# A fused attention, low-rank mix and MLP kernel: float32 low-rank products, copies moved to VectorE, earlier weight decoding, a reordered last hidden layer

## The chip, the cores and the metric

One core of one Trainium2 chip. The metric is device time of one execution in microseconds, the median of the runs.

## The reference

For batch 4, 12 heads, sequence 448 and head size 64, causal attention; its output, with the heads side by side, is x of shape (4, 448, 768). Then a low-rank mix along the sequence and an MLP:

```python
scores = q @ k.T / sqrt(64), masked above the diagonal
attn = exp(scores - max) / (sum + 1e-9);  x = attn @ v
h = x.transpose(0, 2, 1) @ U @ V                 # U (448, 32), V (32, 448)
u = x + h.transpose(0, 2, 1)
out = u + maximum(u @ w_ch1, 0) @ w_ch2          # (768, 3072), (3072, 768)
```

U, V, w_ch1 and w_ch2 arrive as float64 words.

## The kernel before, in words

Everything is computed transposed: x lies as six tiles of 128 channels by 448 positions per batch. Three stages follow one another.

**Attention** (`attention`, line 843 and on). 48 heads pass through a software pipeline of iterations n. `PLAN` (line 47) lists the steps of an iteration in issue order, each with a lag: step (name, lag) works at iteration n on head n - lag. The names: ld loads q and k (L201), ma and mb are the scores (L214; two tiles side by side on the row halves 0 to 63 and 64 to 127), x3 to x0 subtract the maximum (VectorE, L228), e3 to e0 the exponentials (ScalarE, L242), nr the inverse sums (VectorE, L249), n3 to n0 the normalising (POOL, L255), p1, p2, p0 the transposes (L266), h1, h0, h2 the copies of the transposed probabilities out of PSUM (`transposed`, through `copy` L167, engine by the table `ENG`, L39), v the product with v (L281, two heads side by side on column halves), vc its copy. xp transposes x back (L311), xh and xl copy it as a high fp32r part (ScalarE, L315) and the remainder (VectorE, L320); lp is the product with U (`low_rank`, L328: eight fp32r matmuls of 256 columns against a stack of U's high and low parts), lh and ll bring it into the tile y as high part and remainder (L337, L341), once per four heads. `mix` (L346, L347) multiplies y with V's high and low parts, one channel tile per iteration from iteration 14 on for batch 0 and 26 on for batch 1; `mix_sum` (L351) adds it to x, and POOL splits the sum into fp32r parts (L171, L175).

Beside it run steps at fixed iterations: V and U are loaded and decoded from 64-bit words by `low_rank_weights` at iterations -1, 3, 5, 6 (`VU_AT`), and the first two MLP weight blocks are loaded at 10 and 11 and decoded at `START` - 8, 6, 4, 3, 2, that is 26, 28, 30, 31, 32 (`W_AT`). A decoding is two ScalarE passes and three VectorE passes (`decode_bits`, L152 to L156), a sum on POOL (L160) with a store of the block into `kept` (L386), and a split into fp32r parts on ScalarE and VectorE (L178, L179). Such a step is issued right after the first step of its iteration.

**Mixed stage** (`mlp`, lines 402 to 449). From iteration 34 on the MLP of batches 0 and 1 runs, with the rest of the attention steps dealt out between its products at an even rate: products hf (L415) and of (L440), each weight block decoded two blocks ahead. A float32 product is made as three fp32r products of high and low parts.

**Strassen stage** (`strassen`, line 807 and on). Batches 2 and 3 use a seven-product scheme on quads of blocks, with the kept weights loaded again. A quad is (kind, part, k): kind 1 is the hidden layer (9 matmuls per product), kind 2 the output layer (6). There are six parts; hidden quads are called a, b, a2 (part, 0 or 1), output quads k0, k1, k3. `order` (line 725 and on) writes the product sequence; an item (q, n, m) is half of product n. `results` adds each finished product into `xb` (or `r` for kind 1) on VectorE (L461); `hidden` turns a finished hidden quad into operands H, by rounds of VectorE subtractions (tmp, L461), ScalarE casts (L469) and VectorE remainders (h). `prepare` does the same for weights (sw, wsp; L461, L584). `layer` holds the rounds of `hidden`, two per product. `stored` (lines 761 to 767) stores a quad's four tiles in the last part after its seventh product. This stage is ordered by a planner that follows the program order but moves instructions on an engine's queue by its own estimate of readiness; in the stages before the order of the program is kept on every engine.

Of the kernel before, what the change touches and what calls it, by code (L numbers as in the profile page):

```python
# [19 lines left out]
P = 128  # L20
# [19 lines left out]
    "h0": "A", "h1": "A", "h2": "A", "vc": "A",  # L40
# [16 lines left out]
VU_AT = (-1, 3, 5, 6)  # L57
# [8 lines left out]
W_AT = (8, 6, 4, 3, 2)  # L66
# [3 lines left out]
def attention_mix_mlp(ctx: ExitStack, tc: tile.TileContext, qk, v, w1, w2, vu, out):  # L70
# [42 lines left out]
    um_s = const.tile([CP, NT, 4, R], F32R, name="um_s")  # L113
    vm_h = const.tile([P, S], F32R, name="vm_h")
    vm_l = const.tile([P, S], F32R, name="vm_l")
    xn_h = const.tile([CP, NT, 2 * P], F32R, name="xn_h")
    xn_l = const.tile([CP, NT, 2 * P], F32R, name="xn_l")
# [63 lines left out]
    def low_rank_weights(step):  # L181
        if step == 0:
            st["vu"] = load_words(vu, VCOLS)
        elif step == 1:
            st["vua"] = decode_bits(st["vu"], VCOLS)
        elif step == 2:
            decode_sum(st.pop("vu"), st["vua"], VCOLS)
        else:
            a = f(st.pop("vua"))
            split(a[:, :S], vm_h, vm_l)  # L190
            u = a[:CP, S:].rearrange("p (s r) -> p s r", s=NT)
            for i in (0, 2):
                split(u, um_s[:, :, i, :], um_s[:, :, i + 1, :])
# [119 lines left out]
    def natural_high(b, c):  # L313
        cs = slice((c % 2) * P, (c % 2 + 1) * P)
        nc.scalar.copy(xn_h[:, :, cs], st["xn", b, c])  # L315

    def natural_low(b, c):
        cs = slice((c % 2) * P, (c % 2 + 1) * P)
        o = st.pop(("xn", b, c))
        nc.vector.tensor_tensor(xn_l[:, :, cs], o, f(xn_h[:, :, cs]), op=ALU.subtract)  # L320
# [15 lines left out]
    def low_rank_high(b, n):  # L336
        nc.scalar.copy(st["y", b][:, n * 2 * P : (n + 1) * 2 * P], st["yo", b, n])  # L337

    def low_rank_low(b, n):
        y, o = st["y", b][D:, n * 2 * P : (n + 1) * 2 * P], st.pop(("yo", b, n))  # L340
        nc.vector.tensor_tensor(y, o[D:], f(y), op=ALU.subtract)  # L341
# [391 lines left out]
    for p in range(NPART):  # L733
# [150 lines left out]
    with tc.manual_schedule():  # L884
        constants()
        early = [(n, low_rank_weights, (i,)) for i, n in enumerate(VU_AT)]
        early += [(10, load_w, (0,)), (11, load_w, (1,))]
        for n, steps in zip(
# [90 lines left out]
```

## Time and profile before

| | |
|---|---|
| three runs | 913.18 us median (911.19 to 915.44) |
| the profiled execution | 909.54 us, span 907.6 us |
| busy share of the span | TensorE 97%, weight loads 83%, VectorE 73%, ScalarE 54%, POOL 35% |
| mean granted TensorE clock | 0.995 of full speed |

A share of busy time is a mean over stages with different limits; TensorE's ends are modelled, and a record that waits inside a run of merged records counts as busy. So the share alone does not tell what an added operation costs; the rows below are read stage by stage.

### The profile page before, as it was taken

The page shows a single profiled execution, that of the slowest core. Times are in us where ns is not written, and L with a number is a line of the kernel's source. Part 1 is how long each engine was busy: PE and PEld are TensorE (multiplying, and loading weights), DVE is VectorE, ACT ScalarE, POOL GpSimd, SP SyncE. Part 2 cuts the span into 40 slices and gives each one's busy share as a digit, 9 for nine tenths or more (in the row PEclk, how much of TensorE's full clock was granted, in tenths as well). Part 3 has the DMA queues.
Part 4 walks back from the last instruction along what each step waited for, and adds up shares of the span by engine and source line. Part 5 has one row for each costly group of instructions (what it writes and reads, how often), then busy time and mean ns, then how long its engine had stood idle before and what let it go on. Part 6 is the DMA issues. An engine that isn't in the chain of part 4 may idle for free.

```text
span 907.6 us, 13761 instructions
## 1 busy us (share of the span) xinstructions
PE 877.9 (97%) x4728; PEld 749.6 (83%) x4728; DVE 663.6 (73%) x1320; ACT 486.6 (54%) x1050; POOL 314.4 (35%) x342
## 2 busy tenths in 40 slices
PE   6999998999999999999999999899999998999998
PEld 4776766888888888878889999898999897898987
DVE  4656677565665756657568788789888988989885
ACT  5998987654555544455444545364453634445350
POOL 3547576221222322223214425323424323322420
PEclk9999999999999999999999999999999999999999
DMA  8584565354454455433434446612211321202103
GB/s 209 135 216 128 151 156 155 125 174 139 135 179 134 157 165 163 139 116 119 153 105 156 157 157 208 203 42 71 70 52 35 94 59 42 72 24 85 47 1 122
DMA packets 51285, 110.02 MB, mean 121 GB/s; under 512 B 5392, under 2 KB 26896, under 8 KB 51216
## 3 DMA queue, kind: packets, MB, share of 16 engines
q1 hardware_dynamic: 51216, 109.14, 39.7%
q8 instruction: 38, 0.62, 0.3%
q14 instruction: 31, 0.25, 0.1%
HBM read 84.74 MB, written 24.38 MB: 120 GB/s over the span
## 4 chain that ended last, share of the span: by engine, by line
PE 78%; DVE 10%; ACT 7%; issue 3%; DMA 1%; POOL 1%; SPq 0%; DVEq 0%; ACTq 0%; POOLq 0%
PE hf L415 20%; PE of L440 19%; PE sa L647 14%; PE se L647 6%; PE s L214 5%; PE pv L281 5%; PE t L266 4%; ACT p L242 3%; PE sb L647 3%; DVE h L461 2%; DVE tmp L461 2%; DVE sw L461 1%; DVE wsp L461 1%; PE y L328 1%; DVE p L228 1%
## 5 line engine op out<-in xcount | busy, mean ns | idle before, releaser
L440 PE MATMUL of<-g,wsp 128*128 128x448 f32 x864 | 183.8, 368 | 0.0
L461 POOL TENSOR_TENSOR wsp<-wld,wsp 128x512 fp32r<-128x512 f32 (+1 forms) x60 | 104.1, 1745 | 219.2 <-ACT wsp L584 113.2
L440 PEld LDWEIGHTS of<-g,wsp 128*128 128x128 f32 x864 | 160.2, 188 | 18.3 <-issue 2.1
L160 POOL TENSOR_TENSOR wa<-wld 128x768 int32<-128x768 int32 (+1 forms) x49 | 73.2, 1494 | 289.0 <-issue 159.6
L242 ACT ACTIVATE p<-p,m 112x448 f32<-112x448 f32 x192 | 99.7, 523 | 59.6 <-DVE m L228 59.3
L255 POOL TENSOR_SCALAR p<-p,r 112x448 f32<-112x448 f32 x192 | 96.7, 521 | 67.7 <-DVE r L250 40.5
L647 PE MATMUL sa<-h,wsp 128*128 128x448 f32 x432 | 98.5, 367 | 1.4 <-DVE xb L461 0.7
L647 PE MATMUL sa<-uch,wsp 128*128 128x448 f32 x288 | 89.6, 371 | 7.5 <-ACT r L668 4.8
L415 PE MATMUL hf<-u,wsp 128*128 128x448 f32 x432 | 94.9, 370 | 0.0
L415 PE MATMUL hf<-wsp 128*128 128x448 f32 x432 | 94.0, 368 | 0.5 <-ACT pt L167 0.5
L228 DVE CUSTOM_DVE_ANT_0 p<-s,mask 112x448 f32<-112x448 f32 x192 | 75.8, 443 | 20.0 <-PE s L214 19.1
L443 DVE TENSOR_TENSOR xa<-of,xa 128x448 f32<-128x448 f32 x96 | 58.7, 619 | 42.9 <-PE of L440 42.3
L647 PEld LDWEIGHTS sa<-h,wsp 128*128 128x128 f32 x432 | 80.7, 188 | 9.9 <-DVE xb L461 2.0
L415 PEld LDWEIGHTS hf<-u,wsp 128*128 128x128 f32 x432 | 79.8, 188 | 10.7 <-issue 3.8
L415 PEld LDWEIGHTS hf<-wsp 128*128 128x128 f32 x432 | 80.0, 188 | 9.9 <-issue 0.9
L424 DVE SCALAR_TENSOR_TENSOR g<-hf,g 128x448 fp32r<-128x448 f32 x48 | 29.9, 623 | 71.9 <-ACT g L423 71.8
L214 PE MATMUL s<-qk 64*112 64x448 f32 (+3 forms) x384 | 70.5, 444 | 6.6 <-DMA qk<-in_qk_dram 4.2
L178 ACT CAST wsp<-wa 128x768 fp32r<-128x768 f32 x48 | 40.0, 833 | 68.4 <-POOL wa L160 50.9
L423 ACT ACTIVATE g<-hf 128x448 fp32r<-128x448 f32 x48 | 26.1, 543 | 84.0 <-PE hf L415 83.8
L167 ACT COPY pt<-t 112x336 f32<-112x336 f32 x144 | 62.1, 472 | 10.7 <-PE t L266 10.7
L647 PEld LDWEIGHTS sa<-uch,wsp 128*128 128x128 f32 x288 | 54.0, 188 | 16.2 <-ACT r L668 8.3
L584 ACT CAST wsp<-wld 128x512 fp32r<-128x512 f32 (+1 forms) x60 | 41.7, 703 | 47.1 <-PE sa L647 35.7
(92 smaller groups left out, 1598.4 us busy)
## 6 DMA issues: line engine op xcount, KB each, us to landing
wld<-in_w_dram SPq DMA_DIRECT2D x48, 768.0 KB, 4.7
qk<-in_qk_dram SPq DMA_DIRECT2D x96, 224.0 KB, 4.1
kept<-wa SPq DMA_DIRECT2D x48, 384.0 KB, 2.6
wld<-kept SPq DMA_DIRECT2D x24, 384.0 KB, 3.3
wld<-kept SPq DMA_DIRECT2D x72, 128.0 KB, 2.5
v<-in_v_dram SPq DMA_DIRECT2D x24, 224.0 KB, 4.8
out_dram<-xa SPq DMA_DIRECT2D x12, 224.0 KB, 2.3
out_dram<-xb SPq DMA_DIRECT2D x12, 224.0 KB, 1.9
```

Source lines behind the costliest of these rows:

```text
L160: nc.gpsimd.tensor_tensor(a.bitcast(I32), t[:, :n, 1].bitcast(I32), t[:, :n, 0].bitcast(I32), op=ALU.add)
L167: nc.scalar.copy(o, i)
L214: nc.tensor.matmul(o[:, : (i + 1) * CP], t[r, 0, i * CP : (i + 1) * CP], t[r, 1, : (i + 1) * CP], start=True, stop=True,)
L228: nc.vector.tensor_tensor_reduce(out=st["p", b, h][:, POFF[i] : POFF[i] + n], in0=st.pop(("o", b, h, i))[:, :n], in1=mask[:, S - n :], sca ...
L242: nc.scalar.activation(pi, pi, AF.Exp, bias=m[:, i : i + 1], scale=-1.0, accum_out=l[:, i : i + 1])
L255: nc.gpsimd.tensor_scalar(pi, pi, r[:, i : i + 1], 1.0, op0=ALU.mult, op1=ALU.mult)
L281: nc.tensor.matmul(o[j * D : (j + 1) * D, kt * CP : S], v[:, kt, j, :], pt[:, n0 : n0 + S - kt * CP], start=(kt == 0), stop=(kt == NT - 1),)
L415: nc.tensor.matmul(o, a[:, cs], m, start=(kc + n == 0), stop=(kc + n == NC + 1))
L440: nc.tensor.matmul(o, a[:, cs], m, start=(fc + n == 0), stop=(fc + n == FC + 1))
L443: nc.vector.tensor_tensor(x, o, x, op=ALU.add)
L461: (nc.vector if e == "V" else nc.gpsimd).tensor_tensor(o, a, b, op=op)
L647: nc.tensor.matmul(st[bank, q], a, b, start=(n in FIRST and ms[0] == 0 and k == 0), stop=(n in LAST and end and k == len(steps) - 1), skip ...
```

## The change

`ENG` gives h2 to VectorE. The low-rank part keeps U, V, x and y in plain float32: steps xl and ll, the corrections of the high parts, go; lp makes four matmuls of 112 x 32 by 112 x 256 in place of eight of 112 x 128; mix makes one matmul of 32 x 128 by 32 x 448 in place of two of 128 x 128. V and U are loaded at iteration 1 and decoded at 4, 5 and 6; the first two weight blocks are loaded at 3 and 5 and decoded at 8, 9, 10, 11 and 13. The hidden operands of the last part go into tiles of the pool that held the split u of batches 2 and 3, and the second hidden quad of the last part moves from the last part into the one before. Each output tile is stored after the product that completes it.

```diff
 ENG = {
-    "h0": "A", "h1": "A", "h2": "A", "vc": "A",
+    "h0": "A", "h1": "A", "h2": "V", "vc": "A",
...
-    ("xl", 4), ("lv", 1), ("n1", 1), ("xp", 3), ("n0", 1), ("lh", 5),
-    ("ll", 5), ("e1", 0), ("nr", 0),
+    ("lv", 1), ("n1", 1), ("xp", 3), ("n0", 1), ("lh", 5),
+    ("e1", 0), ("nr", 0),
...
-VU_AT = (-1, 3, 5, 6)
+VU_AT = (1, 4, 5, 6)
...
-W_AT = (8, 6, 4, 3, 2)
+W_AT = (8, 9, 10, 11, 13)
...
-            split(a[:, :S], vm_h, vm_l)
-            u = a[:CP, S:].rearrange("p (s r) -> p s r", s=NT)
-            for i in (0, 2):
-                split(u, um_s[:, :, i, :], um_s[:, :, i + 1, :])
+            nc.vector.tensor_copy(vm, a[:R, :S])
+            nc.vector.tensor_copy(um, a[:CP, S:].rearrange("p (s r) -> p s r", s=NT))
...
-        o = st["yo", b, n] = bank("y")[:, : 2 * P]
+        o = st["yo", b, n] = bank("y")[:R, : 2 * P]
         for s in range(NT):
-            for t in (xn_h, xn_l):
-                nc.tensor.matmul(
-                    o,
-                    um_s[:, s].rearrange("p a r -> p (a r)"),
-                    t[:, s, :],
-                    start=(s == 0 and t is xn_h),
-                    stop=(s == NT - 1 and t is xn_l),
-                )
+            nc.tensor.matmul(o, um[:, s], xn[:, s, :], start=(s == 0), stop=(s == NT - 1))
...
-        ys = st["y", b][:, c * P : (c + 1) * P]
-        nc.tensor.matmul(o, ys, vm_h, start=True, stop=False)
-        nc.tensor.matmul(o, ys, vm_l, start=False, stop=True)
+        nc.tensor.matmul(o, st["y", b][:, c * P : (c + 1) * P], vm, start=True, stop=True)
...
         def operand(key):
+            if q[1] == NPART - 1:
+                if not last:
+                    last.extend(p_uc.tile([P, 7, S], F32R, tag=f"u{x}{k}", name="h") for x in "hl")
...
-        if p + 1 < NPART:
+        if p + 2 == NPART:
+            b2 = (1, p + 1, 1)
+            order((a2, 0), (b, 5), (a2, 1), (b, 6), (a2, 2), (a2, 3))
+            order((k0, 0, 0), (k0, 3, 0), (a2, 4), (k0, 1, 0), (a2, 5), (k0, 0, 1), (k0, 3, 1), (a2, 6))
+            order((k0, 2), (k0, 1, 1), (b2, 0), (k0, 4), (b2, 1), (k0, 6), (b2, 2), (k0, 5), (b2, 3), (b2, 4))
+            order((k1, 0), (b2, 5), (k1, 3), (b2, 6), (k1, 2), (k1, 1), (k1, 6), (k1, 4))
...
         else:
-            order((b, 5), (b, 6), (k0, 0, 0), (k0, 3, 0), (k0, 1, 0), (k1, 0, 0), (k1, 3, 0), (k1, 1, 0))
-            order((k0, 0, 1), (k0, 3, 1), (k0, 2), (k0, 1, 1), (k0, 6), (k0, 4), (k1, 0, 1), (k1, 3, 1))
...
+            order((k0, 0), (k0, 3), (k2, 5), (k0, 2), (k0, 1), (k0, 6), (k0, 4), (k1, 0), (k1, 3))
+            order((k0, 5), (k1, 2), (k1, 1), (k1, 6), (k1, 4))
         order((k3, 0), (k3, 3), (k1, 5), (k3, 2), (k3, 1), (k3, 6), (k3, 4))
...
-    def stored(q):
+    def stored(q, n):
         if q[0] == 2 and q[1] == NPART - 1:
-            for d in range(2):
-                for b in range(2):
+            for d, b in {1: ((0, 0),), 4: ((1, 1),), 5: ((0, 1),), 6: ((1, 0),)}.get(n, ()):
...
-                    if q[0] == 2 and q[2] == NC // 2 - 1 and q[1] + 1 < NPART:
+                    if q[0] == 2 and q[2] == NC // 2 - 1 and q[1] + 2 < NPART:
                         layer.extend(hidden((1, q[1] + 1, 0)))
+                    elif q == (1, NPART - 1, 1):
+                        layer.extend(hidden((1, NPART - 1, 0)) + hidden(q))
...
-        early += [(10, load_w, (0,)), (11, load_w, (1,))]
+        early += [(3, load_w, (0,)), (5, load_w, (1,))]
...
-            early += [(START - n, step, a) for step, a in steps]
+            early += [(n, step, a) for step, a in steps]
+        early.sort(key=lambda e: e[0])
```

## Rows read from the trace of the kernel before

**Rows 1.** The chain of waits that ended last, from the page (its part 4): shares of the span by engine. PE is TensorE, PEld its weight loads, DVE VectorE, ACT ScalarE, POOL GpSimd, SP SyncE; a q marks an engine's sequencer.

```profile
PE 78%; DVE 10%; ACT 7%; issue 3%; DMA 1%; POOL 1%; SPq 0%; DVEq 0%; ACTq 0%; POOLq 0%
```

**Rows 2.** The windows view: each stretch in us from the start, its length, then busy us (x instructions) of PE, PEld, DVE, ACT and POOL, the mean granted TensorE clock as a share of full speed, the DMA share and GB/s.

```profile
0.00:35.40 35.40, 26.18 (x165) 18.41 (x165) 17.28 (x78) 25.68 (x82) 15.57 (x33) 0.95 0.74 182
35.40:59.80 24.40, 24.13 (x186) 19.04 (x184) 14.08 (x65) 22.59 (x75) 11.57 (x24) 1.00 0.76 201
59.80:110.50 50.70, 50.23 (x374) 37.44 (x372) 31.26 (x136) 45.64 (x148) 33.06 (x60) 1.00 0.56 140
110.50:151.90 41.40, 37.15 (x255) 25.68 (x253) 31.87 (x99) 34.38 (x105) 29.78 (x46) 0.96 0.59 159
151.90:577.20 425.30, 423.28 (x2229) 363.73 (x2228) 285.23 (x519) 210.95 (x397) 123.43 (x122) 1.00 0.47 152
800.00:858.00 58.00, 57.35 (x280) 52.16 (x279) 52.92 (x82) 26.87 (x46) 16.74 (x10) 1.00 0.19 55
858.00:907.60 49.60, 44.00 (x210) 38.45 (x208) 35.83 (x55) 15.48 (x26) 11.25 (x7) 0.99 0.15 56
```

**Rows 3.** The timeline of iteration 20, from the end of 19 to the start of 21, TensorE's rows: start us, duration us, engine, line, operation, out<-in and count; runs of like instructions are merged.

```profile
85.85 0.47 PE L346 MATMUL hm<-vm_h,y 128*128 128x448 f32 x1
...
86.45 2.11 PE L281 MATMUL pv<-pt,v 112*64 112x448 f32 x16
...
88.49 1.17 PE L266 MATMUL t<-ident,p 112*112 112x112 f32 x10
...
89.59 1.20 PE L214 MATMUL s<-qk 64*112 64x448 f32 x8
...
90.72 0.38 PE L328 MATMUL y<-xn_h,um_s 112*128 112x256 f32 x1
...
91.78 0.60 PE L311 MATMUL xt<-ident,xa 128*112 128x128 f32 x4
...
92.21 1.12 PE L266 MATMUL t<-ident,p 112*112 112x112 f32 x10
```

**Rows 4.** The groups by line with shapes kept apart, whole execution: shapes, count, busy us and mean ns of one, idle before.

```profile
L281 PE MATMUL pv<-pt,v 112*64 112x448 f32 x96 | 26.9, 577 | 1.4 <-ACT pt L167 1.2
...
L281 PE MATMUL pv<-pt,v 112*64 112x112 f32 x96 | 11.1, 265 | 0.0
...
L347 PE MATMUL hm<-vm_l,y 128*128 128x448 f32 x24 | 8.8, 366 | 0.0
```

**Rows 5.** The timeline of TensorE in the mixed stage, around one mix.

```profile
252.56 0.37 PE L346 MATMUL hm<-vm_h,y 128*128 128x448 f32 x1
...
252.96 0.45 PE L266 MATMUL t<-ident,p 112*112 112x112 f32 x3
```

**Rows 6.** The same groups by line as in group 4: a copy of transposed probabilities on ScalarE, a mask pass on VectorE.

```profile
L167 ACT COPY pt<-t 112x336 f32<-112x336 f32 x96 | 42.4, 441 | 5.9 <-PE t L266 5.9
...
L228 DVE CUSTOM_DVE_ANT_0 p<-s,mask 112x336 f32<-112x336 f32 x48 | 24.1, 502 | 0.0
```

**Rows 7.** Iterations 26 to 33: three rows of the timeline (ScalarE, VectorE, TensorE), and two windows with the columns of group 2.

```profile
113.43 0.90 ACT L152 ACTIVATE wa<-wld 128x768 f32<-128x768 f32 x1
...
139.71 2.10 DVE L153 TENSOR_SCALAR wa<-wa 128x768 f32<-128x768 f32 x1
...
141.42 3.77 PE L281 MATMUL pv<-pt,v 112*64 112x448 f32 x16
...
138.00:141.00 3.00, 1.34 (x7) 0.62 (x5) 2.06 (x4) 3.00 (x9) 1.52 (x3) 1.00 0.35 80
141.00:143.00 2.00, 2.00 (x8) 0.80 (x10) 1.97 (x2) 1.02 (x3) 2.00 (x4) 0.68 0.63 158
```

**Rows 8.** The timeline at the start: ScalarE's decoding of V and U, and TensorE's pv that goes on after it.

```profile
17.28 0.71 ACT L152 ACTIVATE wa<-wld 128x576 f32<-128x576 f32 x1
...
19.41 2.10 PE L281 MATMUL pv<-pt,v 112*64 112x448 f32 x14 [1.18 <-ACT pt L167]
```

**Rows 9.** From the page: the DMA issues of weight blocks (KB each, median us to landing), and ahead of it the costliest POOL group of the decoding (columns as in group 4).

```profile
L160 POOL TENSOR_TENSOR wa<-wld 128x768 int32<-128x768 int32 (+1 forms) x49 | 73.2, 1494 | 289.0 <-issue 159.6
...
wld<-in_w_dram SPq DMA_DIRECT2D x48, 768.0 KB, 4.7
```

**Rows 10.** The groups by line of VectorE alone, 858 to 884 us: operands of the last part's hidden quads, and results of the quads before.

```profile
L461 DVE TENSOR_TENSOR h<-tmp,h 128x896 fp32r<-128x896 f32 x4 | 4.4, 1103 | 0.9 <-ACT h L469 0.9
L461 DVE TENSOR_TENSOR h<-r,h 128x896 fp32r<-128x896 f32 x2 | 3.2, 1616 | 0.0
...
L461 DVE TENSOR_TENSOR tmp<-r,tmp 128x448 f32<-128x448 f32 x4 | 2.5, 617 | 0.1
L461 DVE TENSOR_TENSOR h<-r,h 128x448 fp32r<-128x448 f32 x2 | 1.9, 975 | 1.2 <-ACT h L469 1.2
L461 DVE TENSOR_TENSOR xb<-sa,xb 128x448 f32<-128x448 f32 x3 | 1.8, 614 | 0.0
```

**Rows 11.** The timeline of the last part: TensorE after two of its waits.

```profile
875.00 0.47 PE L647 MATMUL se<-uch,wsp 128*128 128x448 f32 x1 [0.77 <-DVE r L461]
...
902.65 1.50 PE L647 MATMUL sa<-h,wsp 128*128 128x448 f32 x6 [0.72 <-DVE xb L461]
```

**Rows 12.** The stores of the last quad, from the view of one tensor (out_dram): duration ns min/median/max, then first and last start in us.

```profile
L765 SPq DMA_DIRECT2D out_dram<-xb x1: 333/333/333, 902.6 to 902.6; - x1
...
L765 SPq DMA_DIRECT2D out_dram<-xb x1: 333/333/333, 904.8 to 904.8; - x1
```

More of the change, by code (lines that the diff above doesn't have):

```diff
@@ L112, in attention_mix_mlp @@
     mask = const.tile([CP, S], F32, name="mask")
[L113 to L117, printed above, removed]
+    um = const.tile([CP, NT, R], F32, name="um")
+    vm = const.tile([R, S], F32, name="vm")
+    xn = const.tile([CP, NT, 2 * P], F32, name="xn")
     def f(ap):
@@ L311, in x_natural, with natural, low_rank_out @@
             nc.tensor.transpose(o[:, s, :], x[:, s * CP : (s + 1) * CP], ident)
-    def natural_high(b, c):
+    def natural(b, c):
         cs = slice((c % 2) * P, (c % 2 + 1) * P)
[L315 to L320, printed above, removed]
+        nc.scalar.copy(xn[:, :, cs], st.pop(("xn", b, c)))
     def low_rank(b, n):
         if n == 0:
-            st["y", b] = p_y.tile([P, DM], F32R, tag="y", name="y")
-        o = st["yo", b, n] = bank("y")[:, : 2 * P]
+            st["y", b] = p_y.tile([R, DM], F32, tag="y", name="y")
+        o = st["yo", b, n] = bank("y")[:R, : 2 * P]
         for s in range(NT):
-            for t in (xn_h, xn_l):
-                nc.tensor.matmul(
-                    o,
-                    um_s[:, s].rearrange("p a r -> p (a r)"),
-                    t[:, s, :],
-                    start=(s == 0 and t is xn_h),
-                    stop=(s == NT - 1 and t is xn_l),
-                )
[L336 to L341, printed above, removed]
+            nc.tensor.matmul(o, um[:, s], xn[:, s, :], start=(s == 0), stop=(s == NT - 1))
+    def low_rank_out(b, n):
+        nc.scalar.copy(st["y", b][:, n * 2 * P : (n + 1) * 2 * P], st.pop(("yo", b, n)))
     def mix(b, c):
         o = st["h", b, c] = bank("hm")[:, :S]
-        ys = st["y", b][:, c * P : (c + 1) * P]
-        nc.tensor.matmul(o, ys, vm_h, start=True, stop=False)
-        nc.tensor.matmul(o, ys, vm_l, start=False, stop=True)
+        nc.tensor.matmul(o, st["y", b][:, c * P : (c + 1) * P], vm, start=True, stop=True)
     def mix_sum(b, c):
@@ L641, in product @@
             else:
-                bh, bl = st["H", m][j]
+                bh, bl = st["H", q[1], m][j]
             cs = slice(m * P, (m + 1) * P)
@@ L696, in hidden @@
         ops = [None] * 7
+        last = []
         def operand(key):
+            if q[1] == NPART - 1:
+                if not last:
+                    last.extend(p_uc.tile([P, 7, S], F32R, tag=f"u{x}{k}", name="h") for x in "hl")
+                h, l = (t[:, UPOS[key]] for t in last)
+                for n in [2] if key == "o" else range(UPOS[key].start, UPOS[key].stop):
+                    ops[n] = last[0][:, n], last[1][:, n]
+                return h, l
             if key == "o":
@@ L712, in end @@
         def end():
-            st["H", k] = ops
+            st["H", q[1], k] = ops
             used.add(("H", q[1], k))
@@ L759, in attention_mix_mlp @@
             units.append(g)
-    def stored(q):
+    def stored(q, n):
         if q[0] == 2 and q[1] == NPART - 1:
-            for d in range(2):
-                for b in range(2):
-                    nc.sync.dma_start(
-                        out=out[2 * q[2] + d, :, (b + 2) * S : (b + 3) * S], in_=xs(q, d, b)
-                    )
+            for d, b in {1: ((0, 0),), 4: ((1, 1),), 5: ((0, 1),), 6: ((1, 0),)}.get(n, ()):
+                nc.sync.dma_start(
+                    out=out[2 * q[2] + d, :, (b + 2) * S : (b + 3) * S], in_=xs(q, d, b)
+                )
     loaded, prepared = [0], [0]
@@ L820, in strassen @@
                 results(q, n)
+                stored(q, n)
                 used.add((q, n))
```

12 lines of the change are left out of this document (5 added, 7 removed).

## The prediction

> **What bounds the kernel now.** I read the chain that ended last, then the windows by stage, then the timeline inside the stages. The chain is TensorE for 78% of the span, VectorE for 10%, ScalarE for 7% [rows 1]. The windows [rows 2] split the span where the work changes: attention alone up to 151.9 us (34 iterations n; the pv products at the top of every even n mark the bounds n = 8, 14 and 26), attention mixed with the first MLP half up to 577.2 us, then the Strassen half. In the mixed stage TensorE is busy 423.3 of 425.3 us: whatever is added there is paid in full.
>
> In attention I compare TensorE's own work with the time it took. From one start to the next, pv takes 2.04 us per pair of heads, the ten transposes 1.10, the scores 1.13, one low-rank product y 1.06, the four xt transposes 0.43, one mix product hm 0.60 [rows 3]. With these, iterations before n = 8 hold 20.6 us in 35.4 (the first load and the filling pipeline cost 14.8), n = 8 to 13 hold 22.9 in 24.4, n = 14 to 25 hold 48.4 in 50.7, n = 26 to 33 hold 33.4 in 41.4. So nearly all stalls lie in the filling and in the last eight iterations, where the weight blocks are decoded. ScalarE is busy 22.6 of 24.4 us in n = 8 to 13: it is as full there as TensorE.
>
> **Part 1, low rank in float32.** Plain float32 matmuls run here already as scores and pv, and each is recorded twice (16 pv records for 8 products). Such a record grows from 265 ns at 112 columns to 577 at 448, 0.93 ns per column, two cycles of 2.4 GHz; one fp32r record of 448 columns takes 366 ns, 211 less, about one trip of 448 columns (187) [rows 4]. One float32 record is thus two trips, a float32 matmul four. Those rows are tiled pairs, though, that can overlap; the untiled product does not occur before. If pairs did not overlap, the price would be half. Scores decide for me: tiles of 448 and 336 columns side by side, then 112 and 224, at four trips and 2.4 GHz take 4 x (448 + 224) / 2.4 = 1.12 us, against 1.13 measured; two trips without overlap, 2 x 1120 / 2.4, would be 0.93. The rule in the Trainium skill, FP8 and Floating Point Precision, section TensorE Precision Notes, is four passes for true FP32; by it the sum is the one below, by two passes it is that of the third rival.
>
> A y call becomes four matmuls of 256 columns: 4 x 4 x 256 / 2.4 = 1.71, with 0.11 for the change of operand 1.82 us, +0.76. Bounds: 0.96 (two trips) and 4 x 2 x 256 x 0.93 + 0.11 = 2.01. A mix becomes one matmul of 448: 0.75, with the restart 0.80 to 0.85 us (bounds 0.46, two trips, and 0.93, 2 x 448 x 0.93 and the restart). It replaces 0.60 in attention and 0.40 in the mixed stage, where hm runs from 252.56 to 252.96 [rows 5]: +0.25 and +0.40. Seven y calls and twelve mixes fall before 151.9: 5.3 + 3.0 = **+8.3 us of TensorE work**. Five and twelve fall in the mixed stage: 3.8 + 4.8 = **+8.6 us**, and nothing there hides it. The removed corrections on VectorE (24 of xn_l, 12 of y) and the casts of U and V save nothing in the mixed stage, since no engine but TensorE is full.
>
> **Part 2, h2 to VectorE.** 48 ScalarE copies of 441 ns leave ScalarE. VectorE gets 48; the nearest row is its 112x336 mask pass out of PSUM, 502 ns [rows 6], the bounds 0.44 (as on ScalarE) and 0.67 (as a pass of 448). On VectorE the copy stands between x3 and x2: behind it wait x2, x0, x1 and the inverse sums, for x2 ScalarE's exp e2. That exp comes some 0.3 us later, inside the 0.44 that ScalarE gained. VectorE is busy 14.1 of 24.4 us and loses xn_l, so it stays clear. Without that cover it would be 0.3 us per head, 10 us in attention; I take nothing.
>
> **Part 3, the filling.** At 17.28 us ScalarE decodes V and U ahead of the copies that pv waits for; pv goes on at 19.41 after 1.18 us idle [rows 8]. That decode moves from n = 3 to 4, the casts at n = 6 shrink to two VectorE copies, and ScalarE loses six h2 copies, 2.6 us. Before n = 8 ScalarE is busy 25.7 of 35.4 us, so about the h2 time and a little more comes back: -3.0 (bounds -4.5 and +1.7). On SP the load of vu moves from n = -1 to 1, those of blocks 0 and 1 from n = 10 and 11 to 3 and 5. A block takes 4.7 us to land [rows 9]; q and k are asked for three iterations (some 12 us) ahead, so I take nothing. If that lead fails, one landing, 4.7 us, is lost once: that is the upper bound.
>
> **Part 4, decoding at n = 8 to 13.** Now it costs most of the 8.0 us stall of n = 26 to 33: ScalarE's pass at 113.43 stands ahead of the pt copies; VectorE's first step at 139.71 took 2.10 us and holds back the masks, and pv at 141.42 takes 3.77 us instead of 2.11, with a granted clock of 0.68 [rows 7]. Moved, the stall in n = 26 to 33 falls to about 0.8, while its products grow by 3.0: -4.2. In n = 8 to 13 TensorE's work is 24.4 us (22.9 + 1.5); ScalarE's is 22.6 less 2.6 for h2, with five decoding passes of about 0.9 (the one at 113.43 took 0.90 [rows 7]), 24.5. Two engines equally full and bursts of two ScalarE passes at the head of its queue: I take a new stall of 4.0 us (bounds 0 and 8, what it costs now) beside 0.4 left of the old 1.5, so +4.4. The sums on POOL (two of 1.49 us [rows 9]) and the stores of kept blocks with the next loads on SP go ahead of the normalising and of q and k; POOL is busy 11.6 of 24.4 us, and the 12 us lead covers SP. Without POOL's cover the transposes come 1.5 us late, twice; inside the bound. In n = 14 to 25 three y and six mixes add 3.8, and ScalarE's relief takes stalls from 2.3 to 1.0: +2.5. **Attention: -3.0 + 4.4 + 2.5 - 4.2 = -0.3 us** (-6 to +5).
>
> **Part 5, the last layer.** Both hidden quads of the last part are now computed within the part before, their operands in the freed u tiles; later products need not be split by m. Now TensorE runs 210 matmuls after 858: at 0.205 each (57.35 / 280) 43.0 us up to 904.15, of 46.1 [rows 2, 11]. The difference, about 3, is VectorE's chain: 0.77 us at 875.00, for example. The 0.72 us before the last product at 902.65 stays [rows 11], the same bank being reused. So 2.4 us are to be had. But both operand chains now start only after product (b2, 6), with 11 products of k1 and k3 left, 66 matmuls, 13.5 us. On VectorE both take 12.0 us by four rows of 858 to 884, and two first subtractions of about 1.1 each (an estimate from the row of the same width) [rows 10], 14.2; less 3.3 not yet needed, 10.9, and nine to eleven results at 0.61 make 16.4 to 17.6, without the weight sums of the next quad. VectorE is busy 52.9 of 58.0 us there already. I take 3.0 us of new stall (bounds 0 and 7): **+0.6 us** (-2.4 to +5).
>
> **Part 6, single stores.** Nothing: the stores already leave as each result is ready, at 902.6 and 904.8 [rows 12]; only one follows the last sum.
>
> **Sum.** -0.3 + 8.6 + 0.6 = +8.9 us. The profiled execution took 909.54 (span 907.6, 1.9 around it), so 918.4. The three runs have a median of 913.18, 3.6 above it; the runs to come are compared with those: **922.1 us**.
>
> **Rivals.**
> (1) ScalarE's relief hides the decoding altogether. Place: n = 2 to 13. For it: ScalarE is full only there, and VectorE's slow decode step ran beside POOL's splitting of x, absent at n = 8. Against: the head-of-queue position stays. Filling -4.5, n = 8 to 13 +0.5, the rest as above: attention -5.7, sum +3.5, 916.7, not slower by what can be told. It decides from the point where the new stall at n = 8 to 13 is under 0.5 us and the first hf begins by 147. Chance 0.22.
> (2) The clock. TensorE idled 1.66 of the 3 us from 138 at the upper clock, 2.4 GHz; in the next 2 us the granted clock was 0.68, so part of them ran at the lower level, 1.2 GHz [rows 7]. If each of the two decode bursts at n = 8 and 11 does that, each costs 1.7 us more, as that pv did: +3.4, 925.5. The rows show it after one burst. The Trainium skill, TensorE: Matmul & The Clock Gate, Part 1: The HAM clock gate, has an idle TensorE fall back to half its clock, which speaks against moving the bursts into a stage that has no stall now. Chance 0.12.
> (3) Untiled float32 costs two trips: y 0.96, mix 0.46. Attention's products then change by 7 x -0.10 and 12 x -0.14, -2.4 in place of +8.3, so attention by -11.0; the mixed stage by +0.2: sum -10.2, 903.0. It decides if pairs do not overlap; against it stands the score row. Chance 0.05.
> (4) VectorE becomes the bound between (b2, 6) and the last part: 7 us of stall, 926. Place and price as in part 5; it decides if the weight sums fall in that stretch. Chance 0.14.
>
> **How the numbers follow.** My own case has 0.47. A difference of 0.5%, 4.6 us, is about what a measurement of this kernel tells from no change. Slower: (2), (4) and 0.41 of my own, 0.67. Same: 0.18 of (1) and 0.06 of my own, 0.24. Faster: (3) and 0.04 of (1), where it meets the lower bounds, 0.09. The range runs from 909 (attention -6, last layer -2.4, mixed stage +4.5, between the two prices of a trip) to 931 (attention +5, last layer +5, mixed stage +8.6, which is 931.8, not all in full); it leaves (3) out.
>
> **What would show it.** Right: y records doubled, eight of about 390 ns per call, hm over 0.75 us; 577.2 reached about 8 us later; the first hf within 4 us of 151.9; VectorE over 95% between (b2, 6) and the last part. Wrong: y under 1.2 us per call; the first hf before 146; the mixed stage no longer than 428 us; TensorE without a gap before the last part's first product.

## The result, and the profile after

The changed kernel takes 924.19 us (four runs, 923.77 to 925.13) against 913.15 (911.19 to 915.44): ratio 1.0121 [1.0096, 1.0146], 1.2% slower, and 2.1 us over the forecast. The profiled execution took 924.43 us, span 922.6, clock 0.997. From one profiled execution to the other that is +14.9 us, since that of before, 909.54, was one of the quicker ones of its kernel.

The share of TensorE in the chain that ended last went from 78% to 83% [rows 1]:

```profile
PE 83%; DVE 9%; ACT 5%; issue 2%; DMA 1%; POOL 0%; SPq 0%; DVEq 0%; POOLq 0%; ACTq 0%
```

The windows of the changed kernel, cut at the first pv, at the pv of n = 8, 14 and 26, at the first hf and at the first Strassen product, and one near the end (columns as in [rows 2]):

```profile
17.27:35.02 17.75, 15.79 (x114) 11.22 (x112) 11.96 (x52) 15.11 (x49) 9.89 (x17) 1.00 0.93 231
35.02:65.24 30.22, 26.74 (x184) 18.48 (x184) 20.33 (x74) 25.88 (x75) 18.31 (x27) 1.00 0.60 163
65.24:120.09 54.85, 54.40 (x374) 35.28 (x372) 30.91 (x138) 43.60 (x136) 32.97 (x61) 1.00 0.56 148
120.09:158.06 37.97, 37.97 (x255) 23.60 (x253) 21.66 (x94) 29.43 (x91) 24.17 (x44) 1.00 0.48 122
158.06:600.69 442.63, 441.66 (x2247) 364.85 (x2245) 289.27 (x524) 204.76 (x380) 125.59 (x123) 1.00 0.44 146
880.00:900.00 20.00, 18.66 (x89) 16.04 (x88) 20.00 (x32) 5.72 (x8) 5.86 (x4) 1.00 0.00 1
```

Cut at the same events the kernel before has 18.11, 24.47, 50.68, 41.38 and 431.55 us, and from the first Strassen product to the last store 321.4 against 319.1. So the 14.9 us are -0.4 (filling), +5.7 (n = 8 to 13), +4.2 (14 to 25), -3.4 (26 to 33), +11.1 (mixed) and -2.3 (Strassen). The mixed stage of before ends with an idle gap of 2.57 us at 583.45, so its true growth is larger: the same window of before, 151.90 to 583.45, holds 426.96 us of busy TensorE, that of after 441.66. The bound of the prediction at 577.2 was not quite that stage's end; these windows replace it.

The new products, by line with shapes apart:

```profile
L318 PE MATMUL y<-xn,um 112*32 112x256 f32 x96 | 23.0, 382 | 0.3 <-ACT xa L165 0.3
L325 PE MATMUL hm<-vm,y 32*128 32x448 f32 x48 | 24.1, 584 | 0.0
L167 DVE COPY pt<-t 112x336 f32<-112x336 f32 x48 | 24.1, 502 | 0.0
```

Two records per matmul and 502 ns for the copy, as the prediction had them. What it did not have stands beside the mix. TensorE's matmuls in the mixed stage of the changed kernel:

```profile
475.60 1.01 PE L325 MATMUL hm<-vm,y 32*128 32x448 f32 x2
476.54 2.09 PE L393 MATMUL hf<-wsp 128*128 128x448 f32 x9
478.56 1.01 PE L325 MATMUL hm<-vm,y 32*128 32x448 f32 x2
479.51 1.91 PE L318 MATMUL y<-xn,um 112*32 112x256 f32 x8
...
486.37 1.77 PE L325 MATMUL hm<-vm,y 32*128 32x448 f32 x4
488.06 2.12 PE L393 MATMUL hf<-u,wsp 128*128 128x448 f32 x9
```

Read from start to next start, one mix takes 0.94 us, two mixes in a row 1.69: the second costs 0.75, four trips of 448 columns at 2.4 GHz (0.747), the first 0.19 more. And the nine fp32r products behind a mix take 2.02 us (476.54 to 478.56) where nine took 1.82 before (459.50 to 461.32). This is the dearest place: over the calls of the stage a mix with the nine behind it takes 0.62 to 0.74 us more than before, a y call with its nine 1.0 to 1.1. The weight loads of the same stretch:

```profile
474.90 0.39 PEld L393 LDWEIGHTS hf<-u,wsp 128*128 128x128 f32 x2
475.60 0.29 PEld L325 LDWEIGHTS hm<-vm,y 32*128 32x128 f32 x2 [0.30 <-issue]
476.54 1.72 PEld L393 LDWEIGHTS hf<-wsp 128*128 128x128 f32 x9 [0.65 <-issue]
```

No weights are loaded ahead of the mix or ahead of the product behind it: each load starts with its own matmul, after 0.30 and 0.65 us in which the loader did nothing. In the kernel before, matmuls and then loads around a mix, both loads start 0.20 us ahead of theirs:

```profile
459.10 0.36 PE L346 MATMUL hm<-vm_h,y 128*128 128x448 f32 x1
...
459.50 1.99 PE L415 MATMUL hf<-wsp 128*128 128x448 f32 x9
461.32 0.28 PE L328 MATMUL y<-xn_h,um_s 112*128 112x256 f32 x1
...
458.90 0.19 PEld L346 LDWEIGHTS hm<-vm_h,y 128*128 128x128 f32 x1
...
459.30 1.81 PEld L415 LDWEIGHTS hf<-wsp 128*128 128x128 f32 x9
```

Last, iterations 11 and 12: decoding's first step on the second block is issued in 11, and the pv of 12 meets what stands behind it. ScalarE, VectorE, TensorE:

```profile
53.07 0.88 ACT L150 ACTIVATE wa<-wld 128x768 f32<-128x768 f32 x1
53.85 0.90 ACT L154 ACTIVATE wld<-wld 128x768 int32<-128x768 uint32 x1
54.66 0.84 ACT L165 COPY pt<-t 112x336 f32<-112x336 f32 x2
...
53.98 0.85 DVE L151 TENSOR_SCALAR wa<-wa 128x768 f32<-128x768 f32 x1 [0.40 <-ACT wa L150]
54.86 0.78 DVE L152 TENSOR_SCALAR wa<-wa 128x768 uint32<-128x768 uint32 x1
55.68 1.08 DVE L153 SCALAR_TENSOR_TENSOR wld<-wld,wa 128x768 uint32<-128x768 uint32 x1
56.69 0.61 DVE L224 CUSTOM_DVE_ANT_0 p<-s,mask 112x448 f32<-112x448 f32 x1
...
57.23 0.50 DVE L167 COPY pt<-t 112x336 f32<-112x336 f32 x1
...
55.12 1.96 PE L277 MATMUL pv<-pt,v 112*64 112x448 f32 x10 [1.68 <-ACT pt L165]
57.78 0.78 PE L277 MATMUL pv<-pt,v 112*64 112x224 f32 x6 [0.70 <-DVE pt L167]
```

pv waits twice: for ScalarE's copies, which stand behind two decoding passes, then for the copy h2, now on VectorE behind three decoding passes and a mask pass.

One pv of the mixed stage, behind passes of a later block, is caught the same way. Its row, and a load of its weights:

```profile
469.50 3.07 PE L277 MATMUL pv<-pt,v 112*64 112x448 f32 x16
...
470.41 0.94 PEld L277 LDWEIGHTS pv<-pt,v 112*64 112x64 f32 x8 [0.72 <-ACT pt L165]
```

The other eight there, and all nine of before, take 2.04 us. So 1.0 us of this row is waiting that counts as busy.

### The profile page after: what moved, and what is told of

Same layout as the page of the kernel before. It is cut to its first block, busy times and chain, and to the rows that moved or that the text cites. A ratio compares the mean times of both kernels' runs of the same rounds, so it can differ in the third digit from the quotient of the medians.

```text
span 922.6 us, 13719 instructions
## 1 busy us (share of the span) xinstructions
PE 900.7 (98%) x4728; PEld 743.1 (81%) x4728; DVE 662.5 (72%) x1331; ACT 475.0 (51%) x999; POOL 316.1 (34%) x342
## 4 chain that ended last, share of the span: by engine, by line
PE 83%; DVE 9%; ACT 5%; issue 2%; DMA 1%; POOL 0%; SPq 0%; DVEq 0%; POOLq 0%; ACTq 0%
PE of L418 19%; PE hf L393 19%; PE sa L625 14%; PE se L625 7%; PE s L210 5%; PE pv L277 4%; PE t L262 4%; PE sb L625 3%; PE hm L325 2%; PE y L318 2%; ACT p L238 2%; DVE h L439 2%; DVE tmp L439 2%; PE xt L307 1%; DVE p L224 1%
## 5 line engine op out<-in xcount | busy, mean ns | idle before, releaser
L439 POOL TENSOR_TENSOR wsp<-wld,wsp 128x512 fp32r<-128x512 f32 (+1 forms) x60 | 106.6, 1785 | 212.9 <-ACT wsp L562 131.7
L224 DVE CUSTOM_DVE_ANT_0 p<-s,mask 112x448 f32<-112x448 f32 x192 | 78.5, 443 | 27.2 <-PE s L210 20.3
L393 PEld LDWEIGHTS hf<-u,wsp 128*128 128x128 f32 x432 | 79.6, 188 | 13.1 <-issue 5.6
L402 DVE SCALAR_TENSOR_TENSOR g<-hf,g 128x448 fp32r<-128x448 f32 x48 | 29.9, 624 | 81.1 <-ACT g L401 81.1
L210 PE MATMUL s<-qk 64*112 64x224 f32 (+3 forms) x384 | 69.0, 444 | 4.5 <-DMA qk<-in_qk_dram 4.2
L625 PEld LDWEIGHTS sa<-uch,wsp 128*128 128x128 f32 x288 | 54.0, 188 | 11.1 <-ACT r L646 6.0
L177 DVE TENSOR_TENSOR wsp<-wa,wsp 128x768 fp32r<-128x768 f32 x48 | 51.5, 1072 | 15.5 <-ACT wsp L176 14.5
L562 ACT CAST wsp<-sw 128x256 fp32r<-128x256 f32 (+3 forms) x60 | 34.0, 578 | 54.6 <-DVE sw L439 25.2
```

The costliest lines, as they stand in the source:

```text
L177: nc.vector.tensor_tensor(lo, src, f(hi), op=ALU.subtract)
L210: nc.tensor.matmul(o[:, : (i + 1) * CP], t[r, 0, i * CP : (i + 1) * CP], t[r, 1, : (i + 1) * CP], start=True, stop=True,)
L224: nc.vector.tensor_tensor_reduce(out=st["p", b, h][:, POFF[i] : POFF[i] + n], in0=st.pop(("o", b, h, i))[:, :n], in1=mask[:, S - n :], sca ...
L393: nc.tensor.matmul(o, a[:, cs], m, start=(kc + n == 0), stop=(kc + n == NC + 1))
L439: (nc.vector if e == "V" else nc.gpsimd).tensor_tensor(o, a, b, op=op)
L625: nc.tensor.matmul(st[bank, q], a, b, start=(n in FIRST and ms[0] == 0 and k == 0), stop=(n in LAST and end and k == len(steps) - 1), skip ...
```

## The experiments

Median us, with the kernel before at 910.9 to 911.2 beside them, and stage lengths of one profiled execution each, cut as above (Strassen: first product to the start of the last store). What lies ahead of the first pv is left out: 18.3 to 18.8 us in e1 to e4, 17.1 to 17.5 in all others. The execution of e9 is its slowest, 904.84: from 472 us to the end of the mixed stage all its products ran 2% slower than those of e10, 2.1 us in sum, and why is open.

| kernel | median | filling | n 8-13 | n 14-25 | n 26-33 | mixed | Strassen |
|---|---|---|---|---|---|---|---|
| before | 911 to 913 | 18.1 | 24.5 | 50.7 | 41.4 | 431.6 | 321.4 |
| after | 924.2 | 17.8 | 30.2 | 54.9 | 38.0 | 442.6 | 319.1 |
| e1 after, fp32r low rank | 906.7 | 17.4 | 29.7 | 52.2 | 35.4 | 428.7 | 320.2 |
| e2 before, float32 low rank | 926.9 | 17.2 | 25.9 | 54.4 | 43.7 | 442.3 | 318.7 |
| e3 after, full tiles | 920.6 | 17.3 | 29.9 | 54.3 | 37.5 | 438.9 | 319.2 |
| e4 after, old decoding | 933.0 | 17.7 | 26.3 | 54.9 | 45.7 | 442.4 | 319.0 |
| e5 after, h2 on ScalarE | 923.2 | 18.3 | 28.4 | 54.4 | 37.7 | 442.6 | 319.9 |
| e6 after, old last layer | 924.8 | 17.4 | 30.2 | 54.8 | 38.0 | 442.4 | 318.9 |
| e7 after, old stores | 924.6 | 17.3 | 30.2 | 54.8 | 38.0 | 442.4 | 319.4 |
| e8 e1, decoding at 14 to 22 | 908.4 | 18.4 | 25.1 | 59.0 | 35.3 | 428.8 | 319.9 |
| e9 e1, h2 on ScalarE | 902.5 | 18.1 | 29.0 | 50.6 | 34.6 | 430.8 | 319.8 |
| e10 e9, one step later | 902.3 | 17.1 | 29.1 | 50.7 | 34.6 | 428.7 | 319.8 |
| e11 before, early decoding | 903.6 | 17.4 | 29.0 | 51.1 | 34.6 | 428.8 | 319.7 |
| e12 e9, only y in float32 | 917.1 | 17.6 | 29.4 | 52.4 | 35.8 | 437.8 | 322.2 |

**e1_fp32r and e2_only_f32: the low rank alone.** e1 puts the changed kernel's low rank back to fp32r, e2 puts float32 into the kernel before:

```diff
-            nc.tensor.matmul(o, um[:, s], xn[:, s, :], start=(s == 0), stop=(s == NT - 1))
+            for t in (xn_h, xn_l):
+                nc.tensor.matmul(o, um_s[:, s].rearrange("p a r -> p (a r)"), t[:, s, :], ...)
```

> The changed kernel with its low-rank part as before (fp32r in high and low parts), all else changed. Changed kernel: 924.2 us; first hf at 158.1; first hf to last y-fed product 442.4. Theory (each float32 mix and y call also slows the fp32r products around it, 0.73 us per mix and 1.0 per y call in the mixed stage, 13.8 in all; attention loses its 8 us of float32 work): the mixed stage goes back to about 428.6, attention ends about 150 to 153, total 902 to 906. Rival A (the four trips alone, 8.6 in the mixed stage; the other 5 come from the new decoding or from h2 on VectorE): mixed stage about 433.5, total about 908 to 910. Rival B (the low rank is not the cause of attention's +6.2, the decoding and h2 are): attention still ends at 157 to 158, total about 910.

> The kernel before with the low-rank part in float32 alone; decoding, h2, last layer and stores as before. Before: 913.2 us, first hf 151.9, mixed stage 428.6. Theory: mixed stage 442.4 (+13.8), attention +6 to +9 (8.3 of TensorE work, some of it in stalls that are there anyway, less the corrections that VectorE sheds), total 933 to 936. Rival A (four trips alone): mixed stage 437, total 928 to 930. If float32 were hidden in attention by its stalls: attention +2 or less, total 927 to 929.

e1: ratio to before 0.9951 [0.9937, 0.9965]; e2: 1.0174 [1.0156, 1.0192]. Float32 costs 17.5 us in the changed kernel (924.2 - 906.7) and 15.7 in the kernel before. The mixed stage agrees with the theory in both: 442.6 against 428.7, 442.3 against 429.0 without the gap. The rival of four trips alone, 8.6, falls. Attention, first pv to first hf, takes 134.6 in e1 (140.8 after) and 141.1 in e2 (134.6 before): float32 costs 6.2 to 6.5 there, at the theory's lower end, and everything else of the change together nothing. The rival for attention falls too. The totals came out lower than the theory had them, in e2 by 6 us (926.9 for 933 to 936): its profile has neither the gap of 2.57 us nor, by 2.7 us, the length of the Strassen stage of before, and the kernel before took 911.2 beside it, not 913.2.

**e3_full_tile: data type or tile size.** Zeros pad the operands to 128 rows and columns:

```diff
-    um = const.tile([CP, NT, R], F32, name="um")
-    vm = const.tile([R, S], F32, name="vm")
+    um = const.tile([CP, NT, P], F32, name="um")
+    vm = const.tile([P, S], F32, name="vm")
```

> The changed kernel with the float32 low-rank operands padded with zeros from 32 to 128 rows or columns, so that y and mix use all of TensorE's rows and columns; same columns streamed. Theory 1 (what disturbs the fp32r products on either side is the change of tile size, 32 rows against 112 and 128): mix start to next start falls from 0.94 to about 0.80 and the nine products behind it from 2.02 to 1.83, mixed stage 442.4 to about 438, total 918 to 920. Theory 2 (it is the change of data type, float32 against fp32r, or the longer fill of float32): unchanged, 924 within 1; if the larger float32 weight load weighs, up to 1 us more per stage.

920.58 us, 3.6 less, with four times the rows or columns in use. The mixed stage loses 3.7 us, attention 1.7; the time ahead of the first pv is 1.5 longer. Matmuls and weight loads around a mix of e3, in this order:

```profile
471.52 0.91 PE L327 MATMUL hm<-vm,y 128*128 128x448 f32 x2
471.93 2.33 PE L395 MATMUL hf<-wsp 128*128 128x448 f32 x9
474.09 0.91 PE L327 MATMUL hm<-vm,y 128*128 128x448 f32 x2
...
471.32 0.40 PEld L327 LDWEIGHTS hm<-vm,y 128*128 128x128 f32 x2
471.90 0.19 PEld L395 LDWEIGHTS hf<-wsp 128*128 128x128 f32 x1 [0.19 <-issue]
```

Now the mix's weights are loaded from 471.32 on, ahead of the mix at 471.52, and those of the next product start 0.03 us ahead of it, at 471.90. Mix and nine products take 0.41 + 2.16 = 2.57 us, with 32 rows 0.94 + 2.02 = 2.96. The split between the two groups was not as theory 1 had it (0.41 and 2.16, not 0.80 and 1.83); their sum bears it out, and the total within 1 us. The Trainium skill, TensorEngine Tiling (Array Packing), section Key Properties, states that a change of tiling mode drains TensorE. The rows agree: with 32 rows no load starts ahead at either border, with 128 rows that of the mix does, and the price here is 3.7 us over 17 calls, 0.22 each. Theory 2 keeps little: with full tiles a mix and its nine are four trips and nine undisturbed products, 0.75 + 1.82 = 2.57, and a y call and its nine take 1.54 + 2.02 = 3.56, against 1.71 + 1.82. TensorE is still busy 437.95 us in the mixed stage, 11.0 more than before. Summed from start to next start, 9.4 of them lie in the calls and in hf and of, where the prediction had 8.6; 1.0 is the one late pv, which e3 has too, and 0.5 lies in the other attention products.

**e4_old_decode, e11_only_decode, e8_mid_decode: when to decode.**

```diff
-W_AT = (8, 9, 10, 11, 13)
+W_AT = (26, 28, 30, 31, 32)     # e4, and loads at 10 and 11; e8 has (14, 16, 18, 20, 22)
```

> The changed kernel with the weight blocks decoded in iterations 26, 28, 30, 31 and 32 again and loaded at 10 and 11, as before. Changed: iterations 8 to 13 take 30.2 us, 26 to 33 take 38.0, first hf at 158.1. Theory (moving the decoding costs what it gives): iterations 8 to 13 back to about 25.5 (-4.7), 26 to 33 up to 41.5 to 44 (+3.5 to +6), first hf at 156.5 to 159.5, total 923 to 926. Rival (the early decoding is a loss, since ScalarE and VectorE are full there): first hf below 155.5, total under 921.5. Rival (early decoding is a gain that the float32 work hides): first hf above 161, total over 927.

> The kernel before with the five decoding steps at n = 8, 9, 10, 11 and 13 and the loads of blocks 0 and 1 at n = 3 and 5, nothing else. Before: 911.1 us; attention from the first pv to the first hf 134.64. With the new last layer, the stores and the load of V and U moved as well (e9_fp32r_h2) it was 902.5 and 132.35. Theory (early decoding is a gain of 2 to 3 us in attention by itself, and it takes away the clock loss that the late bursts cause in attention's end): attention 131 to 132.7, no window at the lower clock at its end, total 902 to 906. Rival (the gain of e9_fp32r_h2 is the new last layer's or the later V and U's): attention 134 or more, total 908 to 911.

> The changed kernel with the low rank in fp32r (run e1_fp32r, 906.7 us: n = 8 to 13 29.67 us, 14 to 25 52.18, 26 to 33 35.35) and the five decoding steps at n = 14, 16, 18, 20 and 22. Theory (decoding at n = 8 to 13 costs since ScalarE is full there, 25.3 of 29.7 us busy and 23 of them without decoding; in n = 14 to 25 it is busy 42.6 of 52.2): n = 8 to 13 back to 25 to 26, n = 14 to 25 52.5 to 54.5, total 903 to 905.5. Rival (a decoding burst costs about 4 us wherever it stands, since its two passes stand at the head of ScalarE's queue and the pv products wait for the copies behind): n = 14 to 25 56 or more, total 906 to 908.

e4 took 933.0 us (927.6 to 933.1): early decoding is a gain of 3.8 us (lowest to lowest) to 8.8 (median to median) in the float32 kernel, the third case, though iterations 8 to 13 moved as the first said. e11: 903.6, ratio 0.9920 [0.9906, 0.9934], attention 132.1: that edit alone takes 7.3 us off the kernel before. Its stages: 26 to 33 -6.8, 8 to 13 +4.6, 14 to 25 +0.4, attention in all -2.5. The span of its profile is 6.9 us shorter than that of before; the rest lies in stages that the edit does not touch, 2.7 in the mixed stage, nearly all of it the gap at its end, and 1.7 in the Strassen stage. e8's rival was nearer, and even it too kind: 8 to 13 gives back 4.6, 14 to 25 takes 6.8, total 1.8 above e1. The late and the middle place have in common what the early one has not, a clock below full. Windows of e4, then of e8:

```profile
140.00:150.00 10.00, 8.57 (x57) 5.46 (x54) 7.80 (x21) 7.92 (x23) 6.23 (x11) 0.99 0.41 110
150.00:162.84 12.84, 12.84 (x67) 7.39 (x65) 8.28 (x26) 7.81 (x25) 8.11 (x11) 0.74 0.61 183
```

```profile
90.00:104.00 14.00, 11.65 (x72) 7.85 (x74) 12.13 (x32) 9.88 (x28) 8.84 (x14) 0.88 0.32 83
```

In e4 TensorE idled 1.43 us of the ten from 140 and then ran at a mean of 0.74, partly at the lower level: 0.26 of 12.84, 3.3 us. That is part of the 7.8 us by which its iterations 26 to 33 are longer than those of the changed kernel; 2.8 are idle time that the changed kernel has not. In e8 the clock is 1.7 (0.12 of 14.00) of the 6.8, idle time 4.9. The kernel before shows the same [rows 7]. In the changed kernel the window 35.02 to 65.24 holds 3.5 us of idle time and reads 1.00.

**e5_h2_act and e9_fp32r_h2: h2 on ScalarE again.**

```diff
-    "h0": "A", "h1": "A", "h2": "V", "vc": "A",
+    "h0": "A", "h1": "A", "h2": "A", "vc": "A",
```

> The changed kernel (924.2 us) with the third copy of transposed probabilities, h2, on ScalarE again. In the changed kernel the pair before n = 8 takes 17.75 us from the first pv, n = 8 to 13 30.22, n = 14 to 25 54.85, n = 26 to 33 37.97, first hf at 158.06. Theory as predicted (h2 on VectorE takes load off a full ScalarE): with h2 back, n = 8 to 13 gets 1 to 3 us longer and the filling 1 to 3, total 926 to 930. Rival (VectorE's masks stand behind h2 and the loop through them sets the pace, so that moving h2 gives nothing or costs): n = 14 to 25 gets 0.5 to 1.5 shorter, n = 8 to 13 within 1 of 30.2, total 922 to 925. The stage from the first hf on should not change by more than 1 either way.

> The changed kernel with the low rank in fp32r and h2 on ScalarE, so that of the change only the early decoding, the load of V and U at n = 1 and 4, the new last layer and the stores are left. With h2 on VectorE it took 906.7 us (n = 8 to 13 29.67, 14 to 25 52.18, 26 to 33 35.35). Theory (h2 on VectorE costs 1 to 2 us, as against the float32 kernel, where putting it back gave 1.8 in n = 8 to 13 and 0.5 in 14 to 25): n = 8 to 13 27.5 to 28.5, n = 14 to 25 50.7 to 51.7, total 904.5 to 906. Rival (with the corrections of the fp32r low rank on VectorE as well, moving h2 to it is worth as much as it costs): within 0.7 of 906.7.

The rival was right in e5, 923.2 us: 8 to 13 gets 1.8 shorter, more than its 1, and 14 to 25 0.5. The medians alone would not settle it (ratio 1.0125 [1.0099, 1.0150] beside 1.0121), but e9 does: 0.9902 [0.9877, 0.9928] against e1's 0.9951 [0.9937, 0.9965], 4.2 us, more than the theory's 1 to 2, with 0.6, 1.6 and 0.8 us less in the three stretches from n = 8 on. The filling gained nothing from h2: it takes 17.1 to 18.4 us in all kernels, in no order (in e5 18.3, of which one late load of v is 1.1). In the fp32r kernel VectorE is fuller, as the corrections run there: busy 23.2 of 29.7 us at n = 8 to 13 of e1, 20.3 of 30.2 in the changed kernel. Most of what h2 costs there lies in iterations 14 to 33, where nothing is decoded. TensorE's longest waits in them in e1:

```profile
PE s L214 <- ACT pt L167: 1.3, 4, 0.5
PE pv L281 <- ACT pt L167: 0.5, 1, 0.5
```

In e9 only one of 0.2 us is left. Why ScalarE's copies come later when it has fewer of them is not shown. At iteration 12 of e5 the second wait is gone:

```profile
54.66 2.53 PE L277 MATMUL pv<-pt,v 112*64 112x448 f32 x16 [1.48 <-ACT pt L165]
```

**e10_shift: the stall's place.** `W_AT = (8, 9, 10, 12, 13)`.

> As e9_fp32r_h2 with the first decoding step of the second block in iteration 12, behind that iteration's pv, and not 11. Theory (what a burst costs depends on its place: at n = 8 its two passes on ScalarE start behind the transposed probabilities that pv waits for, and pv shows no stall; at n = 11 they start ahead of them, and pv of n = 12 waits 1.7 us and 0.7 more): n = 8 to 13 1.5 to 2.5 us shorter than in e9_fp32r_h2, n = 14 to 25 at most 1 longer, total 903 to 905. Rival (the stall only moves to the next step, as the sum on VectorE and POOL follows one iteration behind): total within 0.7 of e9_fp32r_h2.

902.3 us against 902.5: the rival was right. From pv at n = 10 to that at n = 12 it takes 8.19 us in place of 9.75, from there to n = 14 10.43 in place of 8.86: the next pair takes back, with waits of y and the scores, what the first gained.

**e6_old_last and e7_old_store.** e6 takes back `order`, `operand` and the layers of `hidden`, e7 the stores after the seventh product.

> The changed kernel with the order of products and the hidden operands of the last layer as before. From the first Strassen product to the last store the changed kernel takes 319.1 us, the kernel before 321.35, and the kernel before with only the float32 low rank 318.8. Theory (the new last layer is worth nothing by itself; the 2.3 us were one late load of kept weights in that execution of before): 318.3 to 319.3, total 923.5 to 925. Rival (the new order gives 2.4 as its removed stalls promised): 321 to 322, total 926 to 927.

> The changed kernel with the four stores of each last quad issued together behind its last product, as before. Theory: within 0.5 us of 924.2 (the last sum is the same one, one store follows it either way by less than 1 us). Rival (the other three of the last quad's stores now stand ahead of the last one on SyncE, 0.3 us each): 0.6 to 1.5 us longer.

924.8 and 924.6 us: both theories hold. From 840 us on TensorE waits 2.2 us in e6 (three waits) and 2.2 in e7, which has the new order (four waits, the last before the same product).

**e12_y_f32: y without the mix.** Full-tile float32 y, fp32r mix.

> As e9_fp32r_h2 (902.5 us, mixed stage 428.7 without its one stall), with the y product alone in float32 on 128 columns of weights (two of four groups of 32 are zeros), the mix in fp32r with high and low parts of y as before. In the float32 kernel with full tiles (e3_full_tile) a y call took 1.54 us and the nine products behind it 2.02, against 0.96 and 1.83 in fp32r. Theory (the price stays with the call: 0.77 per y call, five in the mixed stage): mixed stage 432.3 to 433, attention 2 to 5 longer, total 908 to 912. Rival (most of the 10.2 that full-tile float32 adds to the mixed stage is the mix): mixed stage 430.5 or less, total under 907.

917.1 us, mixed stage 437.8: neither the theory nor the rival. Each y call took 1.54 us and the nine behind it 2.02, as expected, but TensorE also idled 5.9 us there (2.0 in e11): for VectorE's g 2.2, for a late copy 1.2, at Strassen's start 1.0. Busy time grew by 5.1 (431.90 against 426.79), 1.0 per call. The stage's length tests the price no further; why there are more stalls here is open.

## Why the prediction was right in sum and wrong in its terms

The likeliest case, slower by float32 in the mixed stage, came true, 2.1 us over its time; that the sum came so near is luck. Its terms came out as follows. From one profiled execution to the other it was +14.9 us, not +8.9: attention +6.15 for -0.3, the mixed stage +13.65 without its gap for +8.6, the end with that gap -4.9 for +0.6. The 3.6 us by which the median of before stood over its profiled execution were carried over to the forecast; the changed kernel's median stands 0.2 under its own. So that step, too, was wrong, and it hid most of the other errors. Against the 911 us that the kernel before took beside the experiments the changed one is 13 us slower. Of the signs named, the first hf within 4 us of 151.9 failed: it came at 158.06.

**Part 1, mixed stage: +8.6 was mis-sized, 14.7 of busy time.** The trips were right (y 1.84 us for 1.82, a second mix 0.75). The step that failed is "0.75, with the restart 0.80 to 0.85 us", and that a call's price ends with the call. A mix took 0.94, over the bound of 0.93, and the products behind it paid as well: up to 2.96 us for both, against 2.22 before (0.40 in [rows 5] and 1.82), 0.74 more, with 0.40 forecast. Of the 14.7 us, 13.1 lie in the calls and in hf and of: the 8.6 of the forecast, 3.7 for the tile size (e3), and 0.8 left over. Another 1.0 is the late pv at 469.50, and 0.5 is spread over the other attention products. One stall of before, a mix that waited 1.5 us for VectorE's correction of y, is gone with the correction; the prediction had called the corrections worth nothing there.

**Part 1, attention: +8.3 was 6.2 to 6.5** (e1, e2). The calls cost more than forecast, but part of it fell into stalls that were there.

**Part 2, h2: the term of zero was wrong.** From n = 8 on it costs 2.6 us by e5 and 2.9 by e9. The prediction named the cover (exp later by 0.3 us, ScalarE relieved). Where decoding's passes stand ahead of it on VectorE the copy comes late, and pv waits, 0.70 us of the 1.8 at n = 8 to 13. The cover failed in plain iterations too: 0.8 us by e5 and 2.3 by e9 lie at n = 14 to 33.

**Part 3, the filling: -3.0 was -0.4,** and no run shows a gain there. ScalarE's busy time was taken as the cause; that it fell (16.8 us of 18.1 to 15.1 of 17.75) brought nothing beyond the scatter of that stretch. What sets its pace is not shown.

**Part 4, decoding: the mechanism was right.** +4.4 was +5.7, of which the move alone is 4.6 (e11); -4.2 was -3.4; for 14 to 25, +2.5 was +4.2, since h2 gave no relief (with h2 on ScalarE it is +3.7, e5). Rival 1 (hidden altogether) fell with the first hf at 158.06. Rival 2 (the clock) fell: 1.00 in that window.

**Part 5: +0.6 was +0.2** (319.1 after, 318.9 with the old layer in e6), as less was gained and less lost than forecast, and rival 4 did not come: VectorE is 100% busy from 880 to 900, but TensorE loses 1.2 us to it there, not 7, less than the 3.0 taken too. Against +0.6, the gap before Strassen and the stage itself lost 4.9 us; 4.3 of them are two stalls in the profiled execution of before, TensorE's at 583.45 and, behind a late load on ScalarE, at 764.01:

```profile
583.45 0.45 PE L647 MATMUL sa<-uch,wsp 128*128 128x448 f32 x1 [2.57 <-DVE xa L443]
...
762.50 0.62 ACT L584 CAST wsp<-wld 128x512 fp32r<-128x512 f32 x1 [1.63 <-DMA wld<-kept]
...
764.01 0.47 PE L647 MATMUL sa<-uch,wsp 128*128 128x448 f32 x1 [2.56 <-ACT r L668]
```

The same place in e2, which has the same Strassen stage:

```profile
780.14 0.47 PE L625 MATMUL sa<-uch,wsp 128*128 128x448 f32 x1 [0.83 <-ACT r L646]
```

The first gap stands in no other profile at that size (e12 has 0.98). The second was 1.7 us longer than in e1, e2 and after, but e12 waits 2.13 us at that product. The prediction took the stage's rows as lasting; whether these two are is open. One execution of before was profiled. Without them it would have taken 905 us, but the quickest of the 54 runs of before took 908.5, and e11, which has neither stall, takes 903.6.

**Part 6** was right (e7).

## What to carry to other kernels

A small matmul set between large ones is priced with its neighbours: read from the start of the group ahead to the end of the group behind, and see whether its weights are loaded ahead. Padding it to the tile of its neighbours can be quicker than a smaller one. A burst of decoding is better placed where its stall does not pull the clock down, though the clock was less than half of the difference in e4 and in e8. Early decoding alone, with nothing else of this change, gave 7.3 us, 2.5 of them in attention, and with the rest of the change but float32 and h2 8.7 (e10, 0.9898 [0.9871, 0.9925]).

## What the hardware showed that was not expected

- A float32 mix of 32 rows is dearer than the same of 128 rows with zeros: 2.96 us with the nine products behind it, against 2.57.
- The clock fell after the bursts at 140 (e4, 0.74) and at 90 to 104 (e8, 0.88), not after those at n = 8 to 13, though a pv waited 1.68 and 0.70 us within 3 us of each other there, while the longest wait in e4 ahead of the fall was 1.09. What tells them apart is open.
- The four kept loads at 755.87 of before landed in a median of 4.4 us, in e12 in 4.1, in e1, e2 and after in 3.2. Instruction loads ran near them in before and in after alike, so the cause stays open.
